# Token lists of a routed expert layer: read a block earlier, completed by one-hot products, gathers three tiles ahead

## The chip, the cores and the metric

The kernel runs on one core of a Trainium2 chip. The metric is the device time of one execution in microseconds (us), the median of the runs. The engines are named as in the profile: PE is TensorE, DVE VectorE, ACT ScalarE, POOL GpSimd, SP SyncE, which here only issues transfers.

## What is computed

Three layers in a row on 4608 tokens of 512 features, in float32:

```python
attn_out = attention(q, pooled k, pooled v)          # 8 x 8 heads, 576 queries, keys pooled by 8
x = attn_out.transpose(0, 2, 1, 3).reshape(4608, 512)
h = x @ w_in                                          # 512 -> 2048
x = where(h >= 1, h, where(h <= -1, 0, (h + 1) ** 2 / 4)) @ w_out
logits = x @ w_gate                                   # 8 experts
expert_idx = argmax(logits); gate_w = softmax(logits)[expert_idx]
for e in range(8):
    mask = expert_idx == e
    out[mask] = gate_w[mask] * (maximum(x[mask] @ w1[e], 0) @ w2[e])   # 512 -> 1024 -> 512
```

## The kernel before

Tokens lie in 36 tiles of 128. A float32 product is made as three matmuls on a high and a low part. Attention and the first feed-forward layer run in ten blocks of 3, 4 (seven times), 3 and 2 tiles, numbered 0 to 9: block 8 is the last but one (3 tiles), block 9 the last (2 tiles). A block has 16 steps m; in each, TensorE runs f1 (512 features to 128 hidden ones, lines 476 to 502) two steps ahead and f2 (the hidden ones into the outputs, lines 504 to 512) for step m. A step has two slots, 2m and 2m + 1, into which the other work is dealt: attention of the next block's tiles, and the list todo, of which two entries are taken per slot in blocks 8 and 9. The order on every engine is the order of the program; an engine's queue is worked off in order, but an engine that waits for nothing runs ahead of the place that its code has in the slots. The weights of f2 (WO, 512 KB a step, four buffers) are loaded by ScalarE's queue, one load per step (load_out, line 472).

After a block its tokens are routed (route_steps, from line 522, during the next block): the rows Y are transposed, the logits and the expert are found, s2 works out each token's place in its expert's list (POSF), and writes the rows to yrow_d (SyncE, line 591); s3 then writes the token numbers into perm_d, one indirect scatter of 128 numbers per tile (GpSimd, line 598). Every expert has a list of 4608 places in perm_d, which stands at a padding value at first.

pick_first (block 8, slot 0) takes the expert that has most tokens in blocks 0 to 6, the first expert. Its weights w1 and w2 go into storage that attention uses until then (load_first, eight pieces of 512 KB, SyncE, lines 662 to 669), and are split into high and low parts (cvt1 in slots 13, 15, 18, 21 of block 9, cvt2 from slot 28; some low parts are made by GpSimd, line 226). Its first three tiles (EARLY) are taken from the tokens of blocks 0 to 6. For the tokens of a tile three steps are needed: fetch_ids reads rows of the list with one indirect read (GpSimd, line 648), float_ids converts them (VectorE, line 654), spread_ids transposes them on TensorE so that one token number stands in each partition (lines 659 and 660). Then q_gather gathers the token rows (GpSimd, line 770) and q_tx transposes them for the matmuls (line 778). In slots 2, 7, 9 and 10 of block 9 this is done for the first three tiles, and q_tx is in slots 17, 20 and 23.

The first expert then runs in groups of tiles (f1e and f2e, lines 807 to 831): group 0 with three, then up to eight groups of four. During group 0 the last block is routed, and todo holds after that: the list of the groups of four ("middle"), the tables of the other experts' tiles (table_1, table_2, on VectorE), the list "last" for these, and two gathers. q_turn puts the transposition of the next group's tiles into the last steps of a group. In the last section every other expert's tile is one last_slot: r_gather fetches the tile two ahead, r_tx transposes the next one.

Of the kernel before, what the change touches and what calls it, by code (L numbers as in the profile page):

```python
# [23 lines left out]
def attention_ffn_routed_experts_kernel(  # L24
# [25 lines left out]
    NQ = (NTILE - 4) // 4  # L50
    MAXR = MAXT - 3

    LF, CV1, QT0 = (28, 28, 29, 29, 30, 30, 31, 31), (13, 15, 18, 21), (17, 20, 23)
    EARLY = 3

    BLK = [3] + [4] * 7 + [3, 2]
# [40 lines left out]
    def fx(o, n):  # L97
        return FX[:, o:o + n]
# [79 lines left out]
    RWM = sb.tile([128, 1], I32, name="RWM")  # L178
    TB = sb.tile([128, 8], I32, name="TB")
    GID = sb.tile([128, 4], F32, name="GID")  # L180
    TF = fx(1536, 256)
    IDQ = fx(1792, 128)
    IDM = fx(1920, 4 * NQ).bitcast(I32)
    GIM = fx(1952, 8)
    GIR = fx(1960, 4)

# [327 lines left out]
    def evict_y(j):  # L514
        for t in range(blocks[j][1]):
            if t % 2:
                nc.vector.tensor_copy(Y[:, t, 0:DM], ps[2 + t])
            else:
                nc.scalar.activation(out=Y[:, t, 0:DM], in_=ps[2 + t], func=ACTF.Copy)


    def route_steps(j, bk):
        t0, n = blocks[j]
# [77 lines left out]
        st.append(s1)  # L601
        st.extend([lambda: None] * (5 if j < NB - 2 else 3))
        st.append(s2)
        for t in range(n):
            st.append(lambda t=t: s3(t))
            st.extend([lambda: None] * (0 if t + 1 == n else gap))
        return st


    def e1(lo):  # L610
# [11 lines left out]
    def pick_first():  # L622
        V = nc.vector
        cnt = CB[:, 0]
        mx, mn = MX4[:, 0], MN4[:, 0]
        g = G1[:, 0]
        V.tensor_reduce(out=mx, in_=cnt, axis=AX.X, op=ALU.max)
        V.tensor_scalar(g, cnt, mx, None, op0=ALU.is_equal)
        V.scalar_tensor_tensor(out=g, in0=g, scalar=-16.0, in1=iota4[:, 0], op0=ALU.mult,
                               op1=ALU.add)  # L630
        V.tensor_reduce(out=mn, in_=g, axis=AX.X, op=ALU.min)
        V.tensor_scalar(FST, g, mn, None, op0=ALU.is_equal)
        V.tensor_scalar(FSI, mn, 16.0, None, op0=ALU.add)
        V.tensor_copy(FSR, FSI)

        g3 = POSF[:, 0]
        V.tensor_scalar(g3, FSI, float(NTILE), pcol, op0=ALU.mult, op1=ALU.add)
        V.tensor_copy(RWI, g3)
        V.tensor_scalar(g3, g3, float(EARLY), None, op0=ALU.add)
        V.tensor_copy(RWM, g3)  # L640


    TABS = {"first": (IDR, IDA, EARLY), "middle": (IDQ.bitcast(I32), IDM, 4 * NQ),
            "last": (IDR, IDS, MAXR)}

    def fetch_ids(w):
# [5 lines left out]
    def float_ids(w):  # L652
        r, _, ns = TABS[w]
        nc.vector.tensor_copy(r.bitcast(F32)[0:ns], r[0:ns])
# [7 lines left out]
    def load_first(i):  # L662
        if not first:
            first.append(nc.values_load(FSR[0:1, 0:1], engines=[SP], min_val=0, max_val=NE - 1))
        src = (w1, w2)[i // 4][bass.ds(first[0], 1)].rearrange("o (c p) f -> p (o c) f", p=128)
        if i < 4:
            nc.sync.dma_start(out=ST1[:, i:i + 1], in_=src[:, i:i + 1])
        else:
            nc.sync.dma_start(out=ST2[:, 2 * i - 8:2 * i - 6], in_=src[:, 2 * i - 8:2 * i - 6])
# [177 lines left out]
    def r_gather(j):  # L847
        gather(Y[:, j % 4], r_ids(j))
# [80 lines left out]
    with tc.manual_schedule():  # L929
# [63 lines left out]
        def slot(j, s):  # L993

            want = min(state["units"], -(-(s + 1) * state["units"] // (22 if j == NB - 2 else 29 - 2 * AHEAD + 2)))
            run_units(want - state["done"])
            state["done"] = max(want, state["done"])
            flush()
            if j == 0:
                for _ in range(min(1, PER[s // 2]) if s % 2 == 0 else PER[s // 2] - 1):  # L1000
                    tick()
                if kv:
                    kv.popleft()()
            for _ in range(2 if j >= NB - 2 else 1 + s % 2):
                if todo:
                    todo.popleft()()
            if j == PICK + 2 and s == 0:
                pick_first()
            if j == NB - 2:
                for i in range(8):  # L1010
                    if s == LF[i]:
                        load_first(i)
            if j == NB - 1:
                if s == 2:
                    fetch_ids("first")
                if s == 7:
                    float_ids("first")
                if s == 9:
                    spread_ids("first")
                if s == 10:  # L1020
                    for i in range(EARLY):
                        q_gather(0, i)
                if s in CV1:
                    cvt1(CV1.index(s))
                if s in QT0:
                    q_tx(0, QT0.index(s))
                if s in (28, 30):
                    cvt2(0, (s - 28) // 2, (None, nc.gpsimd)[(s - 28) // 2])
# [38 lines left out]
                nc.sync.dma_start(out=perm_d.rearrange("(p r) o -> p (r o)", p=128), in_=pr)  # L1067
            slot(j, 2 * m + 1)
        evict_y(NB - 1)
        todo.extend(route_steps(NB - 1, bank))  # L1070
        t1, t2 = table_1(), table_2()
        todo.append(lambda: fetch_ids("middle"))
        todo.extend(t1[:12])
        todo.append(lambda: float_ids("middle"))
        todo.extend(t1[12:17])
        todo.append(lambda: spread_ids("middle"))
        todo.extend([lambda i=i: q_gather(1, i) for i in range(4)])
        todo.extend(t1[17:])
        todo.append(lambda: fetch_ids("last"))
        todo.extend(t2[:20])  # L1080
        todo.append(lambda: float_ids("last"))
        todo.extend(t2[20:25])
        todo.append(lambda: spread_ids("last"))
        todo.extend([lambda: r_gather(0), lambda: r_gather(1)])
        todo.extend(t2[25:])
        todo.extend([lambda: fetch_next(0, 0, col=(7, 6)), lambda: fetch_next(0, 1, col=(7, 6))])

        def fill(n):
            for _ in range(n):
# [22 lines left out]
        def step_a(qn):  # L1112
            for m in range(AHEAD):
                f1e(qn, m)
            for m in range(KE // 2):
                f1e(qn, m + AHEAD)
                f2e(qn, m)

        def step_b(qn, more):
            for m in range(KE // 2, KE):  # L1120
# [39 lines left out]
        with tc.If(nq > 0) as some:  # L1160
            middle(1)
        with some.Else():
            first_weights()

        def y_end(j):
# [4 lines left out]
        def last_slot(j):  # L1170
            if_changed(j, lambda: cvt2_half(0), [ACT, DVE])
            fetch_next(j, 1, 0)
            if j + 2 < MAXR:
                r_gather(j + 2)
            u_h(j, 0)
            u_h(j, 1)
            u_th(j % 2, 0, bank())
            if j + 1 < MAXR:
                if_changed(j + 1, lambda: cvt1_half(0), [ACT, DVE])
            if j:  # L1180
                y_end(j - 1)
            if j + 1 < MAXR:
                r_tx(j + 1)
            u_th(j % 2, 1, bank())
            if j + 1 < MAXR:
                if_changed(j + 1, lambda: cvt1_half(1), [ACT, DVE])
                fetch_next(j + 1, 0)
            u_y2(j % 2, 0, ps[4 + j % 2])
            if_changed(j, lambda: cvt2_half(1), [ACT, DVE])
            fetch_next(j, 1, 1)  # L1190
# [46 lines left out]
```

## Time and profile before

| | |
|---|---|
| median of 3 runs | 1578.44 us (1577.69 to 1592.39) |
| the profiled execution | 1580.64 us, span 1578.9 |
| mean granted clock of TensorE | 0.968 of full speed |
| busy share of the span | PE 92%, DVE 50%, ACT 31%, POOL 14% |
| read and written | 171.05 and 28.29 MB, 126 GB/s over the span |

Times in the rows are counted from the start of the span. A row of a timeline gives start, length, engine and line, the operation with what it writes and reads, and in brackets how long the engine had been idle before and what ended it. A row of waits gives who waited for whom, the total, how often and the longest. Matmuls overlap, so their lengths are longer than their distance. In the rows, the blocks have these places: block 8 begins at about 945 us, block 9 at about 1030, the first expert's group 0 at 1097.84, and the last section runs from about 1470 to the end.

### The profile page before, as it was taken

Reading aid. Unit: us, or ns where it says so; the run is one execution under the profiler, and the core shown is the slowest. Engines: PE = TensorE matmul, PEld = TensorE weight load, DVE = VectorE, ACT = ScalarE, POOL = GpSimd, SP = SyncE. Lnnn points to the kernel's source line nnn. Section 1 sums busy time; section 2 is a strip of 40 time slices with the busy share of each in tenths; the row PEclk is TensorE's granted clock in tenths of the full one; section 3 lists DMA queues with packets and bytes.
Section 4 is the critical chain, followed back from the end, with each engine's and each line's share of the span. In section 5 each row is a group of like instructions: output and inputs, shape, how many; then the busy total and the mean of one; then the engine's idle time right before and its main releaser. Section 6 shows DMA issues by size and latency. Waiting matters only on the chain. (4 is left out here: it accounts for less than half of the span.)

```text
span 1578.9 us, 19781 instructions
## 1 busy us (share of the span) xinstructions
PE 1457.9 (92%) x7415; PEld 1185.9 (75%) x7415; DVE 793.5 (50%) x1547; ACT 489.0 (31%) x900; POOL 214.0 (14%) x216
## 2 busy tenths in 40 slices
PE   5677799999999999999999999886699999999797
PEld 4566677778777777777778788775588888888685
DVE  6898756646555654665654445343232222212425
ACT  5344332333332333332333333232111111111334
POOL 4222101001001001001010010002321111111211
PEclk8899999999999999999999999997899999999999
DMA  8566436427629456465475384974141101110403
GB/s 226 161 207 198 134 118 122 127 90 126 131 90 142 122 109 97 130 128 95 132 105 97 100 89 137 201 155 86 41 168 54 54 28 40 44 51 28 159 28 140
DMA packets 102550, 177.28 MB, mean 112 GB/s; under 512 B 46594, under 2 KB 54933, under 8 KB 102432
## 3 DMA queue, kind: packets, MB, share of 16 engines
q10 hardware_dynamic: 21552, 75.79, 24.0%
q1 hardware_dynamic: 73392, 79.93, 17.8%
q0 software_dynamic: 7488, 20.07, 4.3%
q8 instruction: 64, 1.05, 0.3%
q14 instruction: 54, 0.44, 0.1%
HBM read 171.05 MB, written 28.29 MB: 126 GB/s over the span
## 5 line engine op out<-in xcount | busy, mean ns | idle before, releaser
L482 PE MATMUL ps<-XT,W 128*128 128x512 f32 (+2 forms) x640 | 252.1, 394 | 9.1 <-DVE FG L501 8.4
L510 PE MATMUL ps<-WO,FG 128*128 128x512 f32 x576 | 241.6, 419 | 20.2 <-ACT WO L438 10.7
L483 PE MATMUL ps<-XT,W 128*128 128x512 f32 (+2 forms) x640 | 239.9, 375 | 3.0 <-DVE XT L344 3.0
L484 PE MATMUL ps<-XT,W 128*128 128x512 f32 (+2 forms) x640 | 240.0, 375 | 1.5 <-POOL W L226 1.5
L511 PE MATMUL ps<-WO,FG 128*128 128x512 f32 x576 | 230.7, 400 | 3.9 <-POOL WO L226 2.7
L490 ACT ACTIVATE FX<-FX,half 128x512 f32<-128x512 f32 (+2 forms) x152 | 104.0, 684 | 413.7 <-DVE FX L489 406.7
L512 PE MATMUL ps<-WO,FG 128*128 128x512 f32 x576 | 229.9, 399 | 0.0
L489 DVE TENSOR_SCALAR FX<-ps 128x512 f32<-128x512 f32 (+2 forms) x152 | 96.6, 635 | 181.8 <-PE ps L484 181.6
L820 DVE SCALAR_TENSOR_TENSOR FG<-ps,FG 128x512 fp32r<-128x512 f32 (+1 forms) x64 | 43.2, 675 | 220.7 <-ACT FG L819 220.7
L510 PEld LDWEIGHTS ps<-WO,FG 128*128 128x128 f32 x576 | 110.5, 192 | 51.2 <-issue 13.5
L482 PEld LDWEIGHTS ps<-XT,W 128*128 128x128 f32 x640 | 123.5, 193 | 32.0 <-DVE FG L501 9.7
L484 PEld LDWEIGHTS ps<-XT,W 128*128 128x128 f32 x640 | 123.0, 192 | 21.7 <-POOL W L226 2.4
L483 PEld LDWEIGHTS ps<-XT,W 128*128 128x128 f32 x640 | 123.7, 193 | 19.9 <-DVE XT L344 3.9
L495 ACT ACTIVATE FG<-ps 128x512 fp32r<-128x512 f32 (+2 forms) x160 | 88.9, 555 | 148.1 <-DVE ps L494 136.7
L511 PEld LDWEIGHTS ps<-WO,FG 128*128 128x128 f32 x576 | 111.0, 193 | 26.4 <-POOL WO L226 4.1
L512 PEld LDWEIGHTS ps<-WO,FG 128*128 128x128 f32 x576 | 110.6, 192 | 25.1
L494 DVE TENSOR_TENSOR ps<-FX,ps 128x512 f32<-128x512 f32 (+2 forms) x152 | 97.4, 640 | 56.6 <-ACT FX L490 56.6
L501 DVE TENSOR_TENSOR FG<-ps,FG 128x512 fp32r<-128x512 f32 (+2 forms) x160 | 100.8, 630 | 39.7 <-ACT FG L495 39.7
L819 ACT ACTIVATE FG<-ps 128x512 fp32r<-128x512 f32 (+1 forms) x64 | 37.5, 585 | 266.0 <-PE ps L816 265.5
L317 POOL TENSOR_TENSOR AT<-AT,ssm 128x576 f32<-128x576 f32 x36 | 42.6, 1186 | 488.6 <-DVE ssm L310 422.3
L814 PE MATMUL ps<-XT,W 128*128 128x512 f32 (+1 forms) x256 | 99.0, 387 | 0.0
L815 PE MATMUL ps<-XT,W 128*128 128x512 f32 (+1 forms) x256 | 98.6, 385 | 0.0
(215 smaller groups left out, 2281.1 us busy)
## 6 DMA issues: line engine op xcount, KB each, us to landing
WO<-wo_d ACTq DMA_DIRECT2D x144, 512.0 KB
AT<-in_moe_w_dram SPq DMA_DIRECT2D x10, 2048.0 KB
AT<-in_moe_w_dram SPq DMA_DIRECT2D x14, 1024.0 KB
AT<-in_v_dram SPq DMA_DIRECT2D x60, 144.0 KB
AT<-in_q_dram SPq DMA_DIRECT2D x32, 256.0 KB
wo_d<-WO SPq DMA_DIRECT2D x16, 512.0 KB
AT<-in_k_dram SPq DMA_DIRECT2D x56, 144.0 KB
yrow_d<-Y SPq DMA_DIRECT2D x7, 1032.0 KB
```

The lines of the kernel that those rows point to most:

```text
L482: nc.tensor.matmul(o, wi(m, 0, c), xh, start=(c == 0), stop=False)
L483: nc.tensor.matmul(o, wi(m, 0, c), xl, start=False, stop=False)
L484: nc.tensor.matmul(o, wi(m, 1, c), xh, start=False, stop=(c == KD - 1))
L489: nc.vector.tensor_scalar(r, o, -1.0, 1.0, op0=ALU.max, op1=ALU.min)
L490: nc.scalar.activation(out=r, in_=r, func=ACTF.Square, scale=0.5, bias=half)
L494: nc.vector.tensor_tensor(out=o, in0=r, in1=o, op=ALU.max)
L501: nc.vector.tensor_tensor(out=gl, in0=o, in1=r32(gh), op=ALU.subtract)
L510: nc.tensor.matmul(o, gh, WO[:, g % 4, 0], start=(m == 0), stop=False)
L511: nc.tensor.matmul(o, gh, WO[:, g % 4, 1], start=False, stop=False)
L512: nc.tensor.matmul(o, gl, WO[:, g % 4, 0], start=False, stop=(m == KF - 1))
L814: nc.tensor.matmul(o, e1(0)[:, c, ms], xh, start=(c == 0), stop=False)
L815: nc.tensor.matmul(o, e1(0)[:, c, ms], xl, start=False, stop=False)
```

## The change

- The first expert's list of its first three tiles is read, converted, spread and its rows gathered in slots 1, 6, 8 and 9 of block 8 instead of slots 2, 7, 9 and 10 of block 9.
- The middle list is read in slot 17 of block 9, converted in slot 27 and spread in slot 29, as floats (IDMF), when the tokens of blocks 0 to 8 are in perm_d. After the last block's routing, own_1 finds for each of its tokens the row and the column in the list, and builds two one-hot matrices on VectorE; own_2 multiplies them on TensorE and adds the product to IDMF, which gives the list IDM. The four gathers of group 1 follow, and only then the two scatters of the last block, table_1, the reading of the list "last" and table_2. A constant row IO (iota on GpSimd, slot 3 of block 9) is added.
- The list "last" is converted and spread in steps 2 and 3 of group 1, and there three tiles are gathered; in last_slot the tile three ahead is gathered.
- The eight pieces of weights are placed in slots 24, 26, 28 and 30 of block 8 and 0, 2, 4 and 6 of block 9, instead of two each in slots 28 to 31 of block 8.

```diff
-    LF, CV1, QT0 = (28, 28, 29, 29, 30, 30, 31, 31), (13, 15, 18, 21), (17, 20, 23)
+    LF, CV1, QT0 = (24, 26, 28, 30, 32, 34, 36, 38), (13, 15, 18, 21), (17, 20, 23)
+    DEEP = 3
...
+        if j == NB - 1:
+            return st, [lambda t=t: s3(t) for t in range(n)]
...
+    def own_1():
+        V = nc.vector
+        ri, mi, di = RI.bitcast(I32), MD.bitcast(I32), DV.bitcast(I32)
+        V.tensor_scalar(ri, POSF[:, 0:LN].rearrange("p t o -> p (t o)"), POS0, None, op0=ALU.add)
+        V.tensor_scalar(mi, ri, 127, None, op0=ALU.bitwise_and)
+        V.tensor_scalar(di, ri, 7, None, op0=ALU.logical_shift_right)
+        V.tensor_copy(MD, mi)
+        V.tensor_copy(DV, di)
+        V.tensor_tensor(out=VAL, in0=IDF, in1=MD, op=ALU.subtract)
+        for t, (a, b) in enumerate(HOT):
+            V.tensor_scalar(a, IO, MD[:, t:t + 1], None, op0=ALU.is_equal)
+            V.tensor_scalar(b, IO[:, 0:4 * NQ], DV[:, t:t + 1], VAL[:, t:t + 1], op0=ALU.is_equal,
+                            op1=ALU.mult)
+
+    def own_2():
+        pb = bank()
+        for t, (a, b) in enumerate(HOT):
+            nc.tensor.matmul(pb[:, 0:4 * NQ], a, b, start=(t == 0), stop=(t == LN - 1))
+        nc.vector.tensor_tensor(out=IDM, in0=pb[:, 0:4 * NQ], in1=IDMF, op=ALU.add)
...
+        V.tensor_scalar(POS0, FSI, -float(CAP), -float(EARLY * 128), op0=ALU.mult, op1=ALU.add)
+        for t in range(LN):
+            V.tensor_scalar(IDF[:, t:t + 1], pcol, float((blocks[-1][0] + t) * 128 - NT), None,
+                            op0=ALU.add)
...
+            for i in range(8):
+                if 32 * (j - NB + 2) + s == LF[i]:
+                    load_first(i)
             if j == NB - 2:
-                for i in range(8):
-                    if s == LF[i]:
-                        load_first(i)
-            if j == NB - 1:
-                if s == 2:
+
+                if s == 1:
                     fetch_ids("first")
-                if s == 7:
+                if s == 6:
                     float_ids("first")
+                if s == 8:
+                    spread_ids("first")
                 if s == 9:
-                    spread_ids("first")
-                if s == 10:
                     for i in range(EARLY):
                         q_gather(0, i)
+            if j == NB - 1:
+                if s == 3:
+                    nc.gpsimd.iota(IO, pattern=[[1, 128]], base=0, channel_multiplier=0,
+                                   allow_small_or_imprecise_dtypes=True)
+                if s == 17:
+                    fetch_ids("middle")
+                if s == 27:
+                    float_ids("middle")
+                if s == 29:
+                    spread_ids("middle")
...
-        todo.extend(route_steps(NB - 1, bank))
+        st, scatters = route_steps(NB - 1, bank)
         t1, t2 = table_1(), table_2()
-        todo.append(lambda: fetch_ids("middle"))
-        todo.extend(t1[:12])
-        todo.append(lambda: float_ids("middle"))
-        todo.extend(t1[12:17])
-        todo.append(lambda: spread_ids("middle"))
+        todo.extend(st)
+        todo.extend([own_1, lambda: None, own_2])
         todo.extend([lambda i=i: q_gather(1, i) for i in range(4)])
-        todo.extend(t1[17:])
+        todo.extend(scatters)
+        todo.extend(t1)
         todo.append(lambda: fetch_ids("last"))
-        todo.extend(t2[:20])
-        todo.append(lambda: float_ids("last"))
-        todo.extend(t2[20:25])
-        todo.append(lambda: spread_ids("last"))
-        todo.extend([lambda: r_gather(0), lambda: r_gather(1)])
-        todo.extend(t2[25:])
+        todo.extend(t2)
...
+        def last_ids(part):
+
+            if part == 0:
+                float_ids("last")
+            elif part == 1:
+                spread_ids("last")
+                for i in range(DEEP):
+                    r_gather(i)
...
                 f2e(qn, m)
+                if qn == 1 and m > 1:
+                    last_ids(m - 2)
...
-            if j + 2 < MAXR:
-                r_gather(j + 2)
+            if j + DEEP < MAXR:
+                r_gather(j + DEEP)
```

## Rows read from the trace of the kernel before

**Rows 1.** Windows: busy time by engine (number of instructions), then PEclk, DMA share, GB/s.

```profile
100.00:950.00 850.00, 825.17 (x4349) 658.54 (x4346) 512.28 (x968) 298.42 (x537) 80.46 (x77) 0.99 0.55 121
1080.00:1085.00 5.00, 5.00 (x21) 4.61 (x21) 1.61 (x4) 1.13 (x3) 0.00 (x0) 0.50 0.05 21
```

**Rows 2.** Waits of TensorE after 950 us: total, times, longest.

```profile
PE ps L778 <- DMA FX<-yrow_d,IDA: 15.5, 1, 15.5
PE ps L659 <- DVE FX L654: 11.7, 1, 11.7
PE ps L510 <- DMA WO<-wo_d: 7.0, 2, 5.1
PE ps L778 <- DMA Y<-yrow_d,IDS: 5.4, 1, 5.4
```

**Rows 3.** Timeline of TensorE (start, length, what; in brackets idle before and its releaser).

```profile
1007.60 0.76 PE L510 MATMUL ps<-WO,FG 128*128 128x512 f32 x1 [5.15 <-DMA WO<-wo_d]
...
1020.91 0.47 PE L510 MATMUL ps<-WO,FG 128*128 128x512 f32 x1 [1.86 <-DMA WO<-wo_d]
...
1058.44 0.77 PE L510 MATMUL ps<-WO,FG 128*128 128x512 f32 x1 [2.44 <-ACT FX L490]
1059.00 0.63 PE L511 MATMUL ps<-WO,FG 128*128 128x512 f32 x1
...
1079.80 1.12 PE L778 MATMUL ps<-ident,FX 128*128 128x128 f32 x4 [15.50 <-DMA FX<-yrow_d,IDA]
...
1097.84 0.33 PE L814 MATMUL ps<-XT,W 128*128 128x384 f32 x1
...
1115.98 0.34 PE L814 MATMUL ps<-XT,W 128*128 128x384 f32 x1
...
1140.14 0.34 PE L816 MATMUL ps<-XT,W 128*128 128x384 f32 x1
...
1502.07 0.39 PE L879 MATMUL ps<-W,XT 128*128 128x512 f32 x1
```

**Rows 4.** Timeline of GpSimd, block 8 to the first expert.

```profile
982.78 1.01 POOL L598 DMA_INDIRECT perm_d<-idt,POSI  x1 [20.07 <-DVE SM L588]
...
1048.14 1.02 POOL L598 DMA_INDIRECT perm_d<-idt,POSI  x1 [17.03 <-DVE SM L589]
1058.03 0.96 POOL L598 DMA_INDIRECT perm_d<-idt,POSI  x1 [8.88 <-DMA perm_d<-idt,POSI]
1069.03 0.96 POOL L598 DMA_INDIRECT perm_d<-idt,POSI  x1 [10.04 <-DMA perm_d<-idt,POSI]
...
1073.82 2.35 POOL L226 TENSOR_TENSOR W<-AT,W 128x1024 fp32r<-128x1024 f32 x1
...
1125.87 0.99 POOL L598 DMA_INDIRECT perm_d<-idt,POSI  x1 [5.81 <-DMA perm_d<-idt,POSI]
1133.46 0.88 POOL L648 DMA_INDIRECT FX<-perm_d,RWM  x1 [6.61 <-DMA perm_d<-idt,POSI]
```

**Rows 5.** Waits of GpSimd and ScalarE, 940 to 1165 us.

```profile
POOL perm_d L598 <- DMA perm_d<-idt,POSI: 59.5, 6, 11.9
...
ACT FX L490 <- DMA AT<-in_moe_w_dram: 6.9, 1, 6.9
```

**Rows 6.** Timeline of VectorE: row index, end of last routing, list conversion.

```profile
950.73 0.15 DVE L638 CAST RWI<-POSF 128x1 int32<-128x1 f32 x1
...
1116.64 0.17 DVE L590 RECIPROCAL Y<-SM 128x2 f32<-128x2 f32 x1
...
1135.98 0.21 DVE L654 CAST FX<-FX 32x128 f32<-32x128 int32 x1 [12.37 <-DMA FX<-perm_d,RWM]
```

**Rows 7.** Transfers issued on SyncE's (SPq) and ScalarE's (ACTq) queues.

```profile
984.57 2.78 SPq L667 DMA_DIRECT2D AT<-in_moe_w_dram  x4
...
990.58 0.33 ACTq L474 DMA_DIRECT2D WO<-wo_d  x1
...
1049.96 0.33 ACTq L474 DMA_DIRECT2D WO<-wo_d  x1
```

More of the change, by code (lines that the diff above doesn't have):

```diff
@@ L180, in attention_ffn_routed_experts_kernel @@
     GID = sb.tile([128, 4], F32, name="GID")
-    TF = fx(1536, 256)
     IDQ = fx(1792, 128)
     IDM = fx(1920, 4 * NQ).bitcast(I32)
+    IDMF = fx(1964, 4 * NQ)
     GIM = fx(1952, 8)
@@ L519, in evict_y @@
                 nc.scalar.activation(out=Y[:, t, 0:DM], in_=ps[2 + t], func=ACTF.Copy)
+    TF = fx(1536, 256)
     def route_steps(j, bk):
@@ L607, in route_steps @@
         return st
+    LN = blocks[-1][1]
+    POS0 = TF[:, 200:201]
+    IDF = TF[:, 202:202 + LN]
+    RI, MD, DV, VAL = (TF[:, 192 + 2 * i:192 + 2 * i + LN] for i in range(4))
+    IO = WG[:, 5, 0:128]
+    HOT = [(WG[:, 5, 128 + 128 * i:256 + 128 * i], WG[:, 6, 32 * i:32 * i + 4 * NQ])
+           for i in range(LN)]
+    def own_1():
[16 more added lines that the diff above has]
+        nc.vector.tensor_tensor(out=IDM, in0=pb[:, 0:4 * NQ], in1=IDMF, op=ALU.add)
     def e1(lo):
@@ L640, in pick_first @@
         V.tensor_copy(RWM, g3)
-    TABS = {"first": (IDR, IDA, EARLY), "middle": (IDQ.bitcast(I32), IDM, 4 * NQ),
+        V.tensor_scalar(POS0, FSI, -float(CAP), -float(EARLY * 128), op0=ALU.mult, op1=ALU.add)
+        for t in range(LN):
+            V.tensor_scalar(IDF[:, t:t + 1], pcol, float((blocks[-1][0] + t) * 128 - NT), None,
+                            op0=ALU.add)
+    TABS = {"first": (IDR, IDA, EARLY), "middle": (IDQ.bitcast(I32), IDMF, 4 * NQ),
             "last": (IDR, IDS, MAXR)}
@@ L1162, in attention_ffn_routed_experts_kernel @@
         with some.Else():
+            last_ids(0)
+            last_ids(1)
             first_weights()
```

## Prediction

> **What bounds the kernel now.** I read the windows first. Between 100 and 950 us TensorE is busy 825 of 850 us at a clock of 0.99 [rows 1], so nothing can be won there except by removing matmuls, and the change removes none. What is left is where TensorE stands still, and the view of its waits after 950 us gives that by cause [rows 2]: 15.5 us in the last block for the gathered rows of the first expert's first three tiles, 11.7 us for the index list of its next tiles, 7.0 us in two waits for second-layer weights (WO) in block 8, and 5.4 us at a gathered tile in the last section. The timeline of TensorE puts a second price on each [rows 3]: after the stalls of 2.44, 5.15 and 15.5 us matmuls that else take about 0.40 us take 0.63 and more for a while; the windows show the granted clock at 0.50 (the 1.2 GHz level) from 1080 to 1085 [rows 1]. After the stall of 1.86 us the first matmul takes 0.47. I charge half of each slow stretch as loss.
>
> Why are the lists late? The timeline of GpSimd shows it [rows 4]. One token scatter (128 elements of perm_d) waits for the one before: 1048.14, 1058.03, 1069.03, so about 10 us each, 7.6 at the least (1125.87 to the list read it released at 1133.46), and at the most 12.9, the longest such wait (11.9) with the issue before it [rows 5]. What stands behind a scatter on this in-order queue waits too. The three early gathers stand behind all three scatters of block 8; TensorE reaches their tiles at 1064.3 and goes on at 1079.80. The list for the next tiles is read when the last block's two scatters have landed (1133.46), VectorE converts it at 1135.98 [rows 6], and TensorE has then stood 11.7 us.
>
> **First expert's list read in block 8.** The row indices it needs are ready at 950.73 [rows 6], and the scatters of the blocks that it reads from were issued in the block before. GpSimd then sits idle for 20.07 us before 982.78 [rows 4]. Into that gap go one list read and three gathers, four issues of about 1 us with 0.3 between: 5 us in 20, so nothing on TensorE; the later scatters start no later. If that cover were gone, the scatter chain of block 8 would slip by up to 5 us, which no engine waits for before the last block's chain. The list's conversion and its small transposition move with it and cost what they did. So the 15.5 us go, and with them the slow stretch from 1079.80 to 1085 [rows 1, 3]: 5.2 us, half of it 2.6. Removed: 18.1.
>
> What is late next in that place? Two things.
>
> (a) The read of the middle list now stands on GpSimd between the third scatter and the low half of w1's fourth slice, which TensorE needs for the first expert matmul group. Third scatter issued at 1069.03, landing 10 later, 1079; read 0.9; low half 2.4 [rows 4]: 1082.4. TensorE without the 15.5 stall comes there at 1064.3 + (1097.84 - 1079.80) - 2.6 = 1079.7 [rows 3], and needs that slice in the last matmul of the group, eleven of 0.17 (half of the 0.33 in the row, since matmuls overlap) later: 1081.6. Wait: 0.8. With a scatter of 7.6 it is nil; with 12.9 it is 3.7 and a slow stretch. The list itself is converted 2.5 us after its read was issued (1133.46 to 1135.98) [rows 4, 6], at 1081.5, before TensorE gets to its transposition.
>
> (b) The 15.5 us were also a rest in which WO loads caught up. A WO load issued on ScalarE's queue at 1049.96 was used only at 1058.44, 2.44 us late, while a scatter was in flight [rows 3, 7]; nothing else of size was moving but the block's row write. The slow stretch behind it I take as 2.4 us, half of it 1.2 (an estimate; 3.9 is the shortest whose end the rows show). So 3.6 in the 15 us in which block 9 now runs beside scatters. After the change another 10 to 15 us of full-speed steps (1064 to 1079) run beside the second and third scatter. I charge the same once more, 3.6, which also hides the 0.8 of (a). Bounds: 0 (only one of the scatters did it) and 8 (each of the two does it and the first read waits behind it).
>
> Net for this part: 18.1 - 3.6 = 14.5.
>
> **Last block's tokens by one-hot products.** The wait of 11.7 us goes, with the slow stretch to 1140.14 (3.9 us, half is 1.9): 13.6 removed. Added on VectorE: ten small operations behind the routing of the last block, which ends at 1116.64 + 0.17 [rows 6]. Its own chain steps every 0.2 us, so 2.0 us: 1118.8. Two 128-column products follow on TensorE, at most 0.3 each, and one addition. TensorE has finished the second-layer step before them at 1115.98 [rows 3], so it waits 2.8 us. That is beyond the 2.44 after which a slow stretch was seen, so I add 1.2 for one like it, and 0.6 for the products: 4.6. Bounds: 1.8 (operations overlapping, no slow stretch) and 6. The four gathers come 17 us earlier than now, and the two scatters follow them; the list for the last section then stands behind both scatters, ready some 28 us after the products (four issues, two times 10, one read), while it is used only in the second group of tiles, after six more steps of the first group and three of the second. Cost nothing. If that cover failed, TensorE would wait there for what is missing. Net: 13.6 - 4.6 = 9.0.
>
> **Gathers three tiles ahead.** In the last section the third tile's gather is issued only as that section starts, and TensorE waits 5.4 us for it [rows 2]; half speed follows until 1502.07 [rows 3], 5.5 us, half 2.7. In the new order three tiles are gathered in the second group of the first expert, some 300 us earlier, and every later tile one slot earlier. Nothing else is late at that point: the products before the wait had ended, and the activation that the next step needs was there. Net: 8.1, bounds 5.4 and 8.1.
>
> **Weight loads spread.** The eight pieces of the first expert's weights are moved in the program from slots 28 to 31 of block 8 to every second slot from 24 on. But SyncE runs ahead of the program's place: the first four are issued at 984.57 [rows 7], 36 us before TensorE's row at 1020.91 [rows 3], which is step 13 of that block, slots 26 and 27. The order on SyncE's queue (row write of block 7, eight pieces, row write of block 8) is the same before and after, and what each piece waits for is the same storage. So I expect the same issue times, and cost this at nothing. Bounds: what spreading could win at most is the whole of the WO waits in block 8: 7.0 [rows 2] and a slow stretch after 1007.60 like those above, half of it at most 3: 10. What it could lose is bounded by the same wait happening once more, 5.
>
> Here the Trainium skill speaks against the part (DMA: Bandwidth & Descriptors, section Queues, rings and completion order): each DMA engine turns between the queues that have work, packet by packet, so a WO load on one queue should not stand behind the pieces on another, however they are bunched. The trace doesn't bear it out in size: the load issued at 990.58 was used at 1007.60, when TensorE's wait for it ended [rows 3, 7], and ScalarE's next issue waited 6.9 us for a weight piece [rows 5]. By the rule spreading wins 0, by the rows up to 10; it is a reason to keep that rival's chance low.
>
> **Sum.** 14.5 + 9.0 + 8.1 = 31.6, less 0.5 for the extra issues and conversions (an estimate: three operations like the 0.15 at 950.73): 31.1. The profiled execution took 1580.64 (span 1578.9 and 1.7 around it), so 1549.5; it stands 2.2 above the median of the runs, 1578.44, so 1547.
>
> **Rivals.** First, the spread does take effect: 10 us more, 1537. For it, the two WO waits lie exactly where the pieces are in flight; against it, SyncE's order. 0.17.
>
> Second, the stall moves instead of going: every scatter of the last block takes 12.9 instead of 10, so the middle read and the slice behind it come 8.7 us later. TensorE, itself 3.6 late by (b), waits 0.8 + 8.7 - 3.6 = 5.9 for it, and half of a slow stretch, 2; with the one-hot wait at its 6 in place of 4.6 that is 9.3 more, 1556. For it, the list read still hangs on a scatter chain; against it, the chain is 10 us shorter than TensorE's way there. 0.15.
>
> Third, slower than before: in the second half of the last block WO loads set the pace. The load of [rows 7] was issued 6.0 us before the moment at which TensorE asked for it (1058.44 - 2.44 - 1049.96), about two steps of 2.8 us (1079.80 to 1097.84 less 2.6 is five and a half steps with three tiles' transpositions) [rows 3]. If beside scatters each took the 17 us of the load from 990.58 to 1007.60, three in flight, a step would take 5.7 us, 2.9 more, over some 11 steps 32, and as many slow stretches of 1.2 are 13 more: 45 against the 31 won, 1592. It decides from landings of about 14 us on. Against it, the one landing seen in this block took 8.5. 0.04.
>
> Fourth, the change doesn't do what it says: the early read waits for something of block 8 after all and the gathers stay late. Then only the 9.0 and the 8.1 are won: 1561. 0.04. The forecast itself: 0.60, with 1540 to 1555.
>
> **How the numbers follow.** Likeliest 1547. The range takes in the first two rivals and the bounds: 1531 to 1560. A measurement of this kernel can tell about 1% (15.8 us) from no change, so faster means below 1562.7. Faster: the forecast, the first two and most of the fourth, 0.88; within 1%: 0.08; slower by more: 0.04.
>
> **What would show it.** In the changed kernel's waits of TensorE the lines for gathered rows in the last block, for the middle list and for the last section's tile should be gone. A new wait of 2 to 3 us should stand at the one-hot product, waiting for VectorE. In block 9 one or two WO waits of 2 to 3 us, or a wait for w1's fourth slice from GpSimd, stand in the place of the 15.5. The weight pieces should be issued around 985 and 998 us as now, with the WO wait of about 5 us still there; if they come two us apart and that wait is gone, my reading of the order on SyncE is wrong. What would make the prediction wrong is a middle list read more than 5 us after TensorE asks for it.

## The result and the profile after

The changed kernel takes 1565.95 us (median of 4 runs, 1559.5 to 1567.33); the kernel before takes 1584.16 in the 4 runs beside it (1577.69 to 1592.39). The ratio is 0.9883, 95% interval 0.9854 to 0.9912: 1.2% faster, 18 us, where I forecast 31. Two things about the scale. The first three runs of before, whose median 1578.44 I started from, were at the low end: in four later sets of 11 to 17 runs, each on another chip, its median was 1583.6 to 1586.5. Runs of different sets are therefore compared by their ratio to before. And the changed kernel's profiled execution (1567.33, span 1565.6) reached the end of block 1 at 308.0 us, where before's had it at 299.9, in code that the change doesn't touch. Stages are compared by their lengths, not by their places.

The changed kernel, lines by source: the last ACTq row ends block 7, the first weight load of L853 starts group 0, that of L899 the last section.

```profile
L520 ACTq EVENT_SEMAPHORE  x2: 17/17/17, 308.0 to 953.0; - x2
L853 PEld LDWEIGHTS ps<-XT,W x256: 186/188/333, 1089.3 to 1445.5; 128*128 128x128 f32 x128
L899 PEld LDWEIGHTS ps<-W,WO x56: 186/188/189, 1455.5 to 1547.6; 128*128 128x128 f32 x56
```

The same rows of before:

```profile
L519 ACTq EVENT_SEMAPHORE  x2: 17/17/17, 299.9 to 944.8; - x2
L814 PEld LDWEIGHTS ps<-XT,W x256: 187/188/330, 1097.6 to 1459.5; 128*128 128x128 f32 x128
L860 PEld LDWEIGHTS ps<-W,WO x56: 186/188/329, 1469.3 to 1561.5; 128*128 128x128 f32 x56
```

With group 1's first product (1152.9 before, 1138.44 after) and the spans that gives, in us:

| stage | before | after | difference | forecast |
|---|---|---|---|---|
| to the end of block 1 | 299.9 | 308.0 | +8.1 | 0 |
| blocks 2 to 7 | 644.9 | 645.0 | 0 | 0 |
| blocks 8 and 9 | 152.8 | 136.3 | -16.5 | -14.5 |
| group 0 | 55.3 | 49.1 | -6.2 | -9.0 |
| groups 1 and on | 316.4 | 317.1 | +0.7 | 0 |
| last section | 109.6 | 110.1 | +0.5 | -8.1 |

The waits of TensorE after 900 us, changed kernel (total, times, longest):

```profile
PE ps L817 <- DMA out_dram<-WG,FX: 12.0, 1, 12.0
PE ps L511 <- DMA WO<-wo_d: 7.7, 4, 4.2
PE ps L641 <- DVE WG L635: 4.0, 1, 4.0
PE ps L511 <- ACT FG L496: 3.8, 1, 3.8
```

The 15.5, the 11.7 and the 5.4 of [rows 2] are gone, as forecast. A wait of 4.0 stands at the one-hot product, where I had 2.8. WO loads make four waits, one of them 4.2 in block 8 (5.1 before), and the 3.8 stands in block 9 at the same line. At the top is a line that I had nowhere: 12.0 us at a transposition of a gathered tile (L817, r_tx), ended not by a gather but by a write of the output. TensorE's timeline there, and GpSimd's:

```profile
1473.63 1.12 PE L817 MATMUL ps<-ident,Y 128*128 128x128 f32 x4 [11.96 <-DMA out_dram<-WG,FX]
...
1475.26 0.78 PE L918 MATMUL ps<-W,XT 128*128 128x512 f32 x1
...
1476.67 0.39 PE L918 MATMUL ps<-W,XT 128*128 128x512 f32 x1
```

```profile
959.36 0.92 POOL L687 DMA_INDIRECT IDR<-perm_d,RWI  x1 [15.03 <-DVE POSF L674]
...
979.69 1.03 POOL L809 DMA_INDIRECT FX<-yrow_d,IDA  x1 [8.83 <-DVE IDA L699]
...
1087.71 0.90 POOL L687 DMA_INDIRECT FX<-perm_d,RWM  x1 [6.56 <-DMA perm_d<-idt,POSI]
...
1168.05 0.96 POOL L809 DMA_INDIRECT Y<-yrow_d,IDS  x1 [0.31 <-issue]
...
1454.83 0.98 POOL L874 DMA_INDIRECT out_dram<-WG,FX  x1 [32.22 <-DVE WG L873]
1462.89 1.45 POOL L874 DMA_INDIRECT out_dram<-WG,FX  x1 [7.08 <-DMA out_dram<-WG,FX]
1466.93 0.98 POOL L874 DMA_INDIRECT out_dram<-WG,FX  x1 [2.58 <-DMA out_dram<-WG,FX]
1471.47 0.98 POOL L874 DMA_INDIRECT out_dram<-WG,FX  x1 [3.56 <-DMA out_dram<-WG,FX]
```

The tile that L817 transposes was gathered at 1168.05, 306 us earlier. What lies 2 us ahead of its start is the last of the four output scatters of the first expert's last group. By the releaser that the trace names, TensorE waits for transfers that it has no use for, and the matmuls behind take more than 0.39 us until 1476.67. It had reached that place 12.0 us before, at 1461.67. The early steps went as meant: the first list is read at 959.36 and its rows gathered at 979.69, in the gap of [rows 4]; the middle list is read at 1087.71, and no wait hangs on it.

### The profile page after: what moved, and what is told of

It reads as the page before. It is cut to its first block, busy times and chain, and to the rows that moved or that the text cites. A ratio compares the mean times of both kernels' runs of the same rounds, so it can differ in the third digit from the quotient of the medians.

```text
span 1565.6 us, 19805 instructions
## 1 busy us (share of the span) xinstructions
PE 1456.0 (93%) x7419; PEld 1185.2 (76%) x7419; DVE 796.5 (51%) x1561; ACT 488.0 (31%) x900; POOL 220.2 (14%) x218
## 3 DMA queue, kind: packets, MB, share of 16 engines
q8 instruction: 64, 1.05, 0.3%
## 4 chain that ended last, share of the span: by engine, by line
PE 77%; DVE 9%; DMA 6%; issue 3%; ACT 2%; POOL 1%; another core or an unknown queue 1%; SPq 0%; ACTq 0%; DVEq 0%; POOLq 0%
PE ps L483 8%; PE ps L511 7%; PE ps L485 7%; PE ps L484 7%; PE ps L513 7%; PE ps L512 7%; PE ps L853 4%; PE ps L854 4%; PE ps L855 4%; PE ps L868 4%; PE ps L869 4%; PE ps L870 4%; PE ps L339 2%; PE ps L284 2%; DVE FX L428 2%
## 5 line engine op out<-in xcount | busy, mean ns | idle before, releaser
L483 PEld LDWEIGHTS ps<-XT,W 128*128 128x128 f32 x640 | 123.2, 193 | 36.1 <-DVE FG L502 13.9
L853 PE MATMUL ps<-XT,W 128*128 128x512 f32 (+1 forms) x256 | 99.1, 387 | 0.0
## 6 DMA issues: line engine op xcount, KB each, us to landing
AT<-in_v_dram SPq DMA_DIRECT2D x60, 144.0 KB
AT<-in_k_dram SPq DMA_DIRECT2D x56, 144.0 KB
```

The source lines that it names most:

```text
L483: nc.tensor.matmul(o, wi(m, 0, c), xh, start=(c == 0), stop=False)
L853: nc.tensor.matmul(o, e1(0)[:, c, ms], xh, start=(c == 0), stop=False)
```

## The experiments

My theory was that the third part fails by its place. In the change the three gathers stand inside the branch over the number of groups, and the transposition of tile 1 behind it. In the program's instruction list (not in the trace) TensorE's wait there stands on one completion counter, at the value that covers whatever the branch issued on it, the output scatters too. No row shows the counter; what runs can test is the place. In the kernel before the gathers stood outside the branch. The rivals: the rows or their queue are really late; gathering deeper is useless here; the gain was lost in another stage. All results, with stage lengths from the same rows as above:

| run | median, us | ratio to before (95%) | blocks 8, 9 | group 0 | last section |
|---|---|---|---|---|---|
| before | 1583.6 to 1586.5 | 1 | 152.8 | 55.3 | 109.6 |
| changed kernel | 1565.95 | 0.9883 (0.9854 to 0.9912) | 136.3 | 49.1 | 110.1 |
| deep_alone | 1576.38 | 0.9946 (0.9925 to 0.9967) | 154.5 | 56.5 | 101.2 |
| early_alone | 1571.1 | 0.9924 (0.9897 to 0.9952) | 139.4 | 56.4 | 110.9 |
| onehot_alone | 1581.03 | 0.9968 (0.9949 to 0.9988) | 154.2 | 49.1 | 111.8 |
| tail_main | 1563.63 | 0.987 (0.9842 to 0.9899) | 141.2 | 57.9 | 101.4 |
| tx1_inside | 1558.07 | 0.9839 (0.9811 to 0.9868) | 144.0 | 48.1 | 101.1 |
| lf_old | 1565.92 | 0.9887 (0.9859 to 0.9914) | 139.4 | 49.5 | 113.5 |
| pool_later | 1556.23 | 0.9832 (0.9809 to 0.9854) | 141.5 | 45.6 | 103.4 |
| spread_act | 1551.48 | 0.9793 (0.977 to 0.9817) | 137.0 | 48.8 | 101.4 |
| spread_early | 1552.39 | 0.9796 (0.9767 to 0.9825) | 136.5 | 50.8 | 98.1 |
| noscat8 | 1559.41 | 0.9845 (0.9822 to 0.9869) | 134.1 | 49.3 | 113.9 |
| best | 1547.23 | 0.9757 (0.9729 to 0.9785) | 138.7 | 42.0 | 101.1 |

Blocks 2 to 7 take 644.9 to 645.1 in every one. Blocks 8 and 9 of one program vary by some us from one execution to the next (lf_old and the changed kernel, whose queues have the same order, 139.4 and 136.3), so a difference of 3 us there in one profile settles nothing.

**The deeper gathers alone** (deep_alone, on the kernel before):

```diff
-        todo.extend([lambda: r_gather(0), lambda: r_gather(1)])
+        todo.extend([lambda: r_gather(0), lambda: r_gather(1), lambda: r_gather(2)])
...
-            if j + 2 < MAXR:
-                r_gather(j + 2)
+            if j + 3 < MAXR:
+                r_gather(j + 3)
```

> The kernel before with one part of the change: gathers three tiles ahead. Three tiles of the last section are gathered where two were (in group 0 of the first expert, outside any branch), and last_slot gathers three ahead. Theory A (the third part works as I priced it, and fails in the change only because its gathers went inside the branch over the number of groups, so that the transposition of tile 1 behind the branch waits for the output scatters of the first expert's last group): the 5.4 us wait for a gathered tile goes, no wait of about 12 us for out_dram appears, 8 us faster than the kernel before (5 to 8). Rival B (the gathers' transfers are late or the output scatters hold them, wherever they are issued): a wait of 5 to 12 us for a tile or for out_dram stands in the first tile of the last section, 0 to 5 us slower than before.

The last section is 8.4 us shorter, the ratio says 8.6: theory A, and the size that I had priced. Its two longest waits there are now these; neither is for a tile or for the output:

```profile
PE ps L868 <- DVEq L914: 2.5, 1, 2.5
PE ps L860 <- ACT WO L780: 1.7, 1, 1.7
```

**The early list alone** (early_alone: the slots 1, 6, 8, 9 of block 8 in place of 2, 7, 9, 10 of block 9, on the kernel before):

> The kernel before with one part of the change: the first expert's list is read, converted, spread and its rows gathered in block 8 (slots 1, 6, 8, 9). No one-hot products, no deeper gathers, weight pieces where they were. My prediction's term: the 15.5 us wait goes, a wait of 2 to 4 us for second-layer weights (WO) appears in block 9, 14.5 us faster than before; the two profiles of the whole change show 16.5 between the start of block 8 and the first expert's first product. Rival: the part is worth more than the change shows, and the other parts of the change lose it again: over 18 us faster. Other rival: without the middle list read early, the stall moves on to that list, whose wait grows from 11.7 us: under 10 us faster.

Blocks 8 and 9 are 13.4 us shorter, the ratio says 12.1 (7.6 to 16.3). The 11.7 stays what it was (12.0), so the stall didn't move to the middle list; WO waits sum to 10.1 against 9.4 (the 7.0 of [rows 2] and the 2.44 at the same line in [rows 3]).

**The one-hot part alone** (onehot_alone: the changed kernel with the first list's slots of before, the old weight slots, DEEP = 2, and the edit of tx1_inside):

> The kernel before with the second part of the change: the middle list read in block 9, the last block's tokens added by one-hot products, the list of the last section spread in group 1. The first expert's first list and its gathers stay in block 9, the weight pieces where they were, gathers two tiles ahead (the transposition of tile 1 stands inside the branch, so that it doesn't wait for the output scatters). My prediction's term: 9.0 us faster than the kernel before, with a wait of 2.8 us at the one-hot product. The profile of the change shows a wait of 4.0 and 6.7 us between the first expert's first product and that of group 1: by that, 6 to 7 us faster. The 15.5 us wait for the first expert's rows stays.

Group 0 is 6.2 us shorter, as in the changed kernel. The whole gained 5.1 only (1.9 to 8.1). With two tiles ahead the gather of tile 2 is issued behind the output scatters, and TensorE waits 9.9 for it in the last section (5.4 before); in block 9 the wait for the first rows is 18.1 (15.5). The three parts alone add up to 0.54 + 0.76 + 0.32 = 1.6%, with an interval of about 0.4 either way; the changed kernel has 1.2, and tx1_inside 1.6. That fits the account, but wouldn't show it by itself.

**The gathers ahead of the branch** (tail_main, on the changed kernel):

```diff
         q_out(0)
+        last_ids(0)
+        last_ids(1)
         nq = nc.values_load(TB[0:1, 5:6], min_val=0, max_val=NQ)
...
-                if qn == 1 and m > 1:
-                    last_ids(m - 2)
...
```

> The changed kernel, with the list of the last section converted and spread and its three gathers issued at the end of group 0, ahead of the branch, in place of steps 2 and 3 of group 1 inside it. Theory A (a wait behind a branch counts what the branch issued on the same completion counter, and the gathers inside the branch put the output scatters into it): the wait of 12.0 us for out_dram and the slow stretch behind it go, some 13.5 us; against that TensorE waits for the list at the end of group 0, 2 to 5 us with a slow stretch: 8 to 11 us faster than the changed kernel. Rival B (the gathered rows or the queue are late, wherever the gathers stand): the wait of 12 us stays, 2 to 5 us slower than the changed kernel.

The 12.0 is gone and the last section 8.7 us shorter. But the list costs more than I gave it, and group 0 is 8.8 longer:

```profile
1143.62 0.33 PE L698 MATMUL ps<-ident,IDR 40*128 40x40 f32 x1 [6.24 <-DVE IDR L693]
```

So the place of the gathers is what made the wait, and this remedy buys nothing: 8 to 11 us were expected, and the ratio is that of the changed kernel.

**One transposition inside the branch** (tx1_inside, on the changed kernel):

```diff
             r_tx(0)
+            r_tx(1)
...
-            if j + 1 < MAXR:
+            if 0 < j and j + 1 < MAXR:
                 r_tx(j + 1)
```

> The changed kernel, with the gathers left in group 1 and only the transposition of the last section's tile 1 moved: it stands inside the branch, directly behind the transposition of tile 0, near the end of the first expert's last group. Theory A (inside the branch its wait counts only its own gather, which landed long before): the wait of 12.0 us for out_dram and the slow stretch behind it go, nothing is added: 12 to 14 us faster than the changed kernel. Rival B (tile 1's rows really arrive only when the output scatters have run): TensorE waits inside the branch instead, for the gathered rows, about as long: within 3 us of the changed kernel.

The wait is gone, and no other took its place at the transposition. The last section is 9.0 shorter, not 12 to 14, and the ratio says 7: the 12.0 had covered part of other waits there (here 2.0 in three waits, the longest 1.2, with a slow stretch behind it; 3.1 at L868 in the kernel before, 2.5 in deep_alone). With this the place is settled as the cause. In tail_main the reader stays and the gathers leave the branch; here the gathers stay and the reader goes in, some 10 us before TensorE had reached it in the changed kernel, and finds its rows. Neither waits. That it comes about by the counter is read from the program and not shown.

**The weight slots** (lf_old: the old LF in the changed kernel).

> The changed kernel with the weight pieces back in their old slots (two each in slots 28 to 31 of block 8), on SyncE's queue as in both kernels. My prediction costed the spread at nothing, since SyncE runs ahead of the slots: then this is the same as the changed kernel, within 3 us of it, with the pieces issued in the same two bunches, and the wait of 12.0 us for out_dram stays. Rival (the slots do matter): the waits for WO in block 8 grow by 2 us or more and it is 5 to 10 us slower than the changed kernel. As a second use: its stage up to the end of block 1 shows whether the 308 us of the changed kernel's profile (300 in the others) belongs to the kernel or to the run.

The ratio is that of the changed kernel within 0.0004. The pieces go out in the same two bunches; SyncE's queue in the changed kernel:

```profile
993.09 2.79 SPq L706 DMA_DIRECT2D AT<-in_moe_w_dram  x4
996.08 13.22 SPq L708 DMA_DIRECT2D AT<-in_moe_w_dram  x4
```

Its profile has the end of block 1 at 300.8, so the 308.0 belongs to the execution and not to the kernel. Its wait for out_dram was 15.4: the false wait varies.

**A spread that holds** (spread_act, on tx1_inside: load_first issues by nc.scalar.dma_start, the expert's number read on ScalarE; spread_early: the same with LF = (17, 19, ..., 31)).

> The kernel of the run tx1_inside, with the eight weight pieces issued on ScalarE's queue instead of SyncE's, in the same slots. ScalarE's queue carries the activations of the steps, so the pieces can't run ahead of their slots: they should be issued one by one from about 1005 to 1045 us, some 5 us apart, instead of all between 984 and 1000. That is the spread which the change's slots name and its SyncE queue doesn't keep. Theory A (the waits for WO in the second half of block 8, 5.2 and 1.9 us with their slow stretches, come from the pieces in flight together): they go or shrink to under 2 us in sum, 5 to 9 us faster than tx1_inside. Rival B (WO loads are late there for another cause, the scatters for instance): the waits stay within 2 us, and the time within 3. Rival C (the pieces, now ahead of the WO loads on the same queue, delay each of them): the waits grow, slower than tx1_inside by 3 us or more.

> The kernel of the run spread_act, with the eight pieces still on ScalarE's queue, but in every second slot from 17 to 31 of block 8, so that all are issued before the token scatters of block 8 begin (about 1048 us). Theory A (the wait of 7.6 us for WO in block 9 of spread_act comes from its last pieces, which meet the row write and the scatters there): that wait falls to about 3 us as in the other kernels, those in block 8 stay under 4 us in sum, 3 to 5 us faster than spread_act. Rival B (pieces so close together hold the WO loads of block 8 again): waits of 4 us or more come back there, as slow as tx1_inside, 5 to 7 us slower than spread_act.

Now the pieces leave one by one. ScalarE's queue and TensorE in spread_act:

```profile
1011.07 0.36 ACTq L706 DMA_DIRECT2D AT<-in_moe_w_dram  x1
1014.49 0.35 ACTq L706 DMA_DIRECT2D AT<-in_moe_w_dram  x1
...
1039.89 0.40 ACTq L708 DMA_DIRECT2D AT<-in_moe_w_dram  x1
```

```profile
1020.68 0.47 PE L511 MATMUL ps<-WO,FG 128*128 128x512 f32 x1 [1.73 <-DMA WO<-wo_d]
1030.39 0.50 PE L511 MATMUL ps<-WO,FG 128*128 128x512 f32 x1 [1.83 <-DMA WO<-wo_d]
1056.57 0.77 PE L511 MATMUL ps<-WO,FG 128*128 128x512 f32 x1 [7.56 <-DMA WO<-wo_d]
```

Theory A holds for block 8: of 5.2 and 1.9 only the 1.73 at 1020.68 is left there. The other two waits lie in block 9, whose second step begins at 1030.39 (two tiles follow there, not three). The ratio is 0.0046 below tx1_inside's: 7 us, with an interval of about 1 to 13. Where the gain lies is seen from the row in which ScalarE takes block 8's first result, in tx1_inside and then in spread_act:

```profile
1030.95 0.60 ACT L520 ACTIVATE Y<-ps 128x512 f32<-128x512 f32 x1 [1.27 <-PE ps L513]
```

```profile
1021.66 0.60 ACT L520 ACTIVATE Y<-ps 128x512 f32<-128x512 f32 x1 [0.76 <-PE ps L513]
```

Counted from the end of block 7 to that row, block 8 takes 84 to 87 us in all ten profiles with the pieces on SyncE's queue and 76 in the three with them on ScalarE's. From there to group 0, block 9 takes 60 to 63 in these three, against 52 to 57 in the kernels with the early list and the pieces on SyncE's queue (noscat8 left aside). So block 8 gains more than the whole, and block 9 gives much of it back: there a wait of 7.6 came in spread_act. In spread_early it fell to 3.7, but waits of 3.1 and 3.0 stand elsewhere in block 9; WO waits sum to 11.8 against 13.9, and the time is the same. So its theory A has this wait right and the gain of 3 to 5 us wrong, and rival B didn't come true.

What made block 8 shorter, the place of the pieces or their queue, these two runs don't separate. Two readings bear on it. The busy share of the DMA engines from 985 to 1008 us is 1.05 in tx1_inside, 0.74 in spread_act and 0.91 in spread_early. And in each of the ten profiles with the pieces on SyncE's queue ScalarE, which issues the WO loads, itself stands 6.2 to 8.5 us for one of the pieces (6.9 in [rows 5]); with the pieces on its own queue that wait is gone.

**Block 9 without scatters** (noscat8, on tx1_inside: s3 left out for block 8).

> The kernel of the run tx1_inside without the three token scatters of block 8, so that the tokens of that block are missing from the lists and from the output; the number of tiles and steps stays the same. My step (b) was that WO loads are late beside scatters. If that holds, the waits for WO in block 9 (3.3 us and the later ones of 1 to 4 us) go, those of block 8 beside the weight pieces (5.2 and 1.9) stay, and block 9 gets 4 to 8 us shorter. If the WO waits of block 9 have another cause (the row write of block 8, the order of the loads), they stay: less than 2 us.

TensorE's waits from 1045 to 1100 in tx1_inside, and then in noscat8:

```profile
PE ps L511 <- DMA WO<-wo_d: 3.3, 1, 3.3
PE ps L483 <- DVE FG L502: 2.1, 1, 2.1
```

```profile
PE ps L544 <- ACT WG L538: 1.5, 2, 0.8
PE ps L483 <- DVE FG L502: 1.4, 1, 1.4
```

No WO wait is left beside the routing of block 8: its scatters are what makes these loads late (one profile of noscat8; each of the others has such a wait, 2.4 to 7.6). Block 9 takes 47.5 us, against 52 to 57 with the scatters, and the waits of block 8 beside the pieces stay (5.3, 1.9). (Only this stage of noscat8 is read; without block 8's tokens its gathers and output scatters differ.) The second line has another cause, which the next run names.

**GpSimd's low half later** (pool_later, on tx1_inside):

```diff
-            if m < 2:
-                cvt2(1, m, (None, nc.gpsimd)[m])
+            if m in (0, 2):
+                cvt2(1, m // 2, (None, nc.gpsimd)[m // 2])
```

> The kernel of the run tx1_inside, with one thing moved: GpSimd's low half of the last second-layer slice (cvt2, 2.35 us) in step 2 of group 0 instead of step 1. In the traces of the change that operation runs beside one small VectorE operation of the routing chain which takes 2.35 us instead of 0.17, and the one-hot operations stand behind it. Theory A (VectorE is held while GpSimd works on that slice): the small operation takes 0.2 us again, the wait at the one-hot product falls from 4.0 to about 1.8 us, the slow stretch behind it shrinks: 2 to 3.5 us between the first expert's first product and that of group 1. Rival B (that operation is long for another reason, its operands for instance): it takes 2.35 us still, the wait stays 4.0, no gain.

VectorE in the changed kernel, where GpSimd's L227 runs from 1107.61 for 2.35 us, and then in pool_later:

```profile
1107.56 0.17 DVE L586 COPY CB<-CB 128x8 f32<-128x8 f32 x1
1107.64 2.35 DVE L587 TENSOR_TENSOR G<-G,ebase 128x16 f32<-128x16 f32 x1
1110.02 0.17 DVE L588 TENSOR_TENSOR G<-G,OH 128x16 f32<-128x16 f32 x1
```

```profile
1105.75 0.17 DVE L587 TENSOR_TENSOR G<-G,ebase 128x16 f32<-128x16 f32 x1
```

Theory A: 2.35 became 0.17, the wait at the product 1.85, and group 0 is 2.5 shorter than in tx1_inside. 16 numbers in each partition took as long as GpSimd's operation, and ended with it. This is the rule of the Trainium skill (SBUF — State Buffer, section SBUF: two separate sides): a VectorE operation with two inputs in SBUF and a GpSimd operation that reads SBUF share a port pair as an exclusive lock; the one that starts first has it for its whole instruction, and the other stands still. The rows agree: the operation held reads G and ebase, both in SBUF, and GpSimd's started first, at 1107.61 against 1107.64. The whole, at 0.9832, isn't told apart from tx1_inside; 2.7 us of the false wait show again in its last section, at tile 2, which is transposed behind the branch too.

**All of it** (best: the changed kernel with the edits of tx1_inside, pool_later and spread_act, and own_2 five entries later in todo).

> The edits that the runs favoured, together on the changed kernel: the transposition of tile 1 inside the branch (as tx1_inside), GpSimd's low half one step later (as pool_later), the one-hot product five list entries later, behind the next first-layer group of about 2.1 us, and the weight pieces on ScalarE's queue in the change's own slots (as spread_act). If the gains add: no wait at the one-hot product (1.85 us was left in pool_later), 43 to 44 us between the first expert's first product and that of group 1, about 137 us for blocks 8 and 9, 101 to 103 for the last section: a span of about 1546, a ratio to the kernel before of 0.976 to 0.978. If they don't add (the gathers of group 1 or the lists come late for the later product): a new wait for gathered rows in the last steps of group 0, no faster than spread_act at 0.979.

The gains add: no wait at the product, group 0 in 42.0, the last section in 101.1, 2.4% faster than before (2.1 to 2.7) and the fastest of all; its span of 1545.3 is about what I had forecast for the change, but by other gains: the pieces on ScalarE's queue and the two edits at the one-hot product are not in that forecast. Block 9 still has a WO wait of 5.1.

## Why the prediction was wrong, point by point

**Gathers three tiles ahead: this step failed.** I wrote that three tiles are gathered in the second group, some 300 us earlier, that "Nothing else is late at that point", and took 8.1. The size was right (deep_alone 8.4, tail_main 8.7, tx1_inside 9.0). What failed is that the gathers' new place is inside a branch and their reader behind it. I followed when the data would be there, and not what the reader's wait would take in. A wait of 12.0 took the place of the 5.4 and of the 3.1 behind it: +0.5 instead of -8.1, the largest part of the miss, and none of my four rivals was this one.

**One-hot products: right mechanism, one term mis-sized.** The wait of VectorE was 4.0 instead of 2.8, and 2.2 of it was GpSimd's hold on VectorE, which I hadn't looked for. The change brought it about. In the kernel before, GpSimd's low half stood behind the last block's first scatter in its queue, and VectorE's operation was done by then:

```profile
1115.54 0.17 DVE L584 TENSOR_TENSOR G<-G,ebase 128x16 f32<-128x16 f32 x1
```

```profile
1117.63 2.42 POOL L226 TENSOR_TENSOR W<-AT,W 128x1024 fp32r<-128x1024 f32 x1
```

With the scatters moved behind it, it starts at 1107.61, beside that operation. Without the hold the wait is 1.85, under my 2.8, since the ten operations step faster than 0.2 us. Group 0 gained 6.2 to 7.4 (the trace of before has 55.3, deep_alone and early_alone 56.5 and 56.4), against 9.0; with the edit of pool_later 9.7.

**Early list: right, within what one profile can tell.** 14.5 forecast; 16.5 in the two profiles, 13.4 alone, and 8.8 to 13.4 in the profiles of tx1_inside, tail_main, pool_later and lf_old. The charge for what would be late next is borne out: WO loads beside the scatters (noscat8), 3.3 to 3.9 us in one wait that before had too (2.4), and behind it something of 1 to 4 more. In tx1_inside that second wait is partly the hold again: VectorE's low half of a w1 slice takes 3.43 us from 1073.64, beside GpSimd's of 2.39 from 1073.59, and TensorE waits 2.1 behind it. In noscat8 the two don't meet; it takes 1.23 and the wait is 1.4. In before GpSimd's ran inside the 15.5 us stall [rows 4] and VectorE's behind it. The 0.8 for the fourth slice doesn't appear.

**Weights spread at nothing: right** (lf_old). The change's isn't a spread. The rival was right in what it bounded: with the pieces issued one by one from ScalarE's queue block 8 loses 8 to 11 us, where I had 10 at most, but block 9 takes much of it back: by the ratio 7 us remain, by the lengths of the two blocks 3 to 7. The packet-by-packet turns that I cited from the Trainium skill (DMA: Bandwidth & Descriptors, section Queues, rings and completion order) would, as I read them, have made it worth nothing; spread_act speaks against that reading, though it also moves the pieces to the queue of the WO loads. With the DMA engines busy throughout (a share of 1.05), a load can be late though they take turns.

**The base.** 1578.44 was 5 to 8 us low; that shifts the predicted time, not the difference. By the table of stages, 31.6 less 8.6 (gathers), 2.8 (one-hot) and 0.7, and 2.0 more in blocks 8 and 9, leaves 21.5 behind block 1 (the 0.5 for extra issues doesn't show); the medians give 18.

**The chances.** The forecast, the first two rivals and most of the fourth are 0.60, 0.17, 0.15 and nearly 0.04, about 0.95 for faster, and not the 0.88 that I wrote. The measured 1565.95 lies within 1% of 1578.44, to which I gave 0.08.

## What to carry to other kernels

When a transfer moves into a branch, look at who waits for it behind the branch: the wait may take in other transfers that the branch issued, and a gather issued 306 us before can cost 12 us. Put the reader on the same side as the transfer. Where a slot in the program is meant to set a transfer's time, check that its queue is kept to that place: SyncE ran ahead by 36 us, ScalarE's queue held the place, and the whole got about 7 us shorter. Before a stall is removed, or an operation is moved off GpSimd's queue, look at which operations of VectorE and GpSimd were kept apart by it.

## What the hardware showed that I had not expected

A VectorE operation on 16 numbers per partition took 2.35 us instead of 0.17, and one of 1.23 took 3.43, each for a GpSimd operation that ran at the same time. The time to the end of block 1 was 298.8 to 302.5 us in eleven profiles and 308.0 and 309.3 in two, by the same code; what delays it was not tried. In the changed kernel, an output scatter of 128 rows of 2 KB held GpSimd's next by 2.6 to 7.1 us in the first expert's last group; a token scatter of 128 numbers of 4 bytes did so by 6.6 to 13.2 from block 8 on, mostly about 10.
